# q and k laid out by head channel, and another order of TensorE's work, in a kernel of windowed attention beside a gated MLP

## The chip, the cores and the metric

The kernel runs on one NeuronCore of a Trainium2 chip. The core has five engines, each with its own instruction stream: TensorE (PE; its weight loads are listed apart as PEld), VectorE (DVE), ScalarE (ACT), GpSimd (POOL) and SyncE (SP). Each engine runs its stream in order and waits for others on semaphores. Transfers are issued from the queues of SP, ACT and POOL and run on 16 shared DMA engines. The metric is the time of one execution on the device, in microseconds (us). The runs of the kernel before took 208.5 us in the median (208.3 to 209.07, three runs).

## What is computed

`x` holds 2048 tokens of 512 channels in bf16. Two branches of the normalised tokens are added to it:

```python
xn = _layernorm(x)
# A: 32 heads of 16 channels; a token looks at itself and at 7 tokens before it, two apart
q, k, v = split_heads(xn @ wqkv)
logits = einsum('bhsd,bhswd->bhsw', q, kg) * 16 ** -0.5   # kg: k at s, s-2, ..., s-14
o = einsum('bhsw,bhswd->bhsd', softmax(mask(logits)), vg)
A = o @ wo
# B: a gated MLP that mixes over tokens
z = gelu(xn @ w_in)                                        # 512 -> 1376
z1, z2 = z[..., :688], _layernorm(z[..., 688:])
g = einsum('ts,bsf->btf', w_sp, z2) + b_sp                 # 2048 x 2048
B = (z1 * g) @ w_out                                       # 688 -> 512
out = x + A + B
```

## The kernel before

The tokens are taken in 16 tiles of 128. The program is written with its order by hand: a list of short names for TensorE and ScalarE (`ten`, L418) and one for VectorE (`vec`, L411), which a small loop (`advance`, L604) goes through in order, pulling from the other list what a name needs. Each engine's stream comes out in that order.

*Token tiles.* `s` takes the statistics of a tile (L163), `r` or `R` the inverse root (on POOL, L167, or on ACT for the first two), `n` normalises on VectorE (L175). Tiles 0 to 3 are turned by TensorE (`T`, L180, copied out at L181), tiles 4 to 15 by a DMA transpose from the SP queue (`t`, L184). The result is `xnT`, channels on partitions.

*z2 and z1.* `z` projects a token tile to the second half of z (L190: eight matmuls of 128x344 into a buffer `mm`, of which there are three, two PSUM banks each), `h` is its gelu on ScalarE with a running sum (L196), `q` its square on ScalarE (L201). `zs` makes mean and inverse root for four tiles (L207 to L211), `zn` normalises a z2 tile on VectorE (L217). `y` is a z1 tile: the same L190 and a gelu at L222.

*q and k.* `k` projects chunks (L230): eight matmuls of 128x128 weights on 512 tokens for two of the four groups of channels of q or of k. A partition then holds one of four channels of a head, so a head's 16 channels lie on four partitions and in four groups of the free dimension. ACT copies them out (L232).

*Logits.* For each half `th` of the tokens and each pair of window offsets `w2`: `m` multiplies q by k shifted by the offset (L262, two operations of 4096 elements per partition), `f` and `p` add the four groups (L263, L264; for some pairs the first add is a DMA with accumulation from POOL, `d`, L270), and `S` sums over the four partitions of a head on TensorE with a selector matrix (L276), copied by ACT into `a_sb` with the scale (L278). Now a partition is (quarter of the tokens, head), 32 heads times 4 quarters.

*Softmax and attention.* `x` maximum and subtraction (L286 to L290), `e` exponential on ACT (L294), `u` sum (L299 to L301), `i` inverse by logarithm and exponential on ACT (L305, L306), `c` scaling (L310). `v` projects v in the layout (quarter, head) at once: 32 columns of weights for one channel of all heads, four such matmuls side by side in the array (L245). `H` copies the last 16 tokens of a quarter to the next one, as halo, by DMA (L250, L251). `a0.0` to `a0.11` and `a1.0` to `a1.11` are attention's products and sums for the two halves on VectorE (L318, L322, L331); `.11` writes the output.

*Mixing, gate, output.* `W` loads and transposes 256 rows of w_sp (L338, SP queue) into one of three buffers. `M` mixes one tile (L345: 32 matmuls), ACT adds the bias (L348) into one of three buffers, `g` multiplies by z1 on VectorE (L353) and issues the transpose of the result from SP (L357, or L359 and L360). `Q0` to `Q3` are the four groups of four output tiles (L385 and L390 for the gated part, L396 for attention); `F` adds x and stores (L401, L402). The first half's output groups come before the second's.

In `ten` four z2 tiles are followed by the projections of q and k of the first half, and then z2 tiles, projections, v, z1 and mixing tiles alternate.

## Time and profile before

| | |
|---|---|
| median of three runs | 208.5 us (208.3 to 209.07) |
| span of the profiled execution | 207.7 us, from the first to the last instruction |
| granted TensorE clock | 1.000 |
| DMA | 29.79 MB, 143 GB/s in the mean |

The profiled execution is one run; its span leaves out what lies before the first and after the last instruction, and the page gives no other time for it. The span stands 0.8 us below the median. In groups of instructions a row reads: line, engine, operation, out<-in, shapes, count, then busy us, mean ns of one, and the idle time of the engine before them with what ended it. Durations of neighbours overlap a little, so the pitch of back-to-back work is read from starts.

### The profile page before, as it was taken

The numbers are of one execution on the slowest core, as the hardware profiler recorded it, in microseconds if no ns is written. First come the engines' busy times: TensorE is split into PE (matmuls) and PEld (weight loads), VectorE is DVE, ScalarE is ACT, GpSimd is POOL, SyncE is SP. The second block draws the span as 40 slices with busy tenths as digits, with TensorE's granted clock in tenths as the row PEclk, the third lists the DMA queues.
The fourth block names the chain that finished last, engine by engine and source line by source line (L and its number), as shares of the span: only waits on it lengthen the run. The fifth ranks groups of instructions, "written<-read, shape, count | busy, mean of one in ns | idle before, by whom it ended". The sixth has DMA issues, their size and how long they took to land.

```text
span 207.7 us, 3772 instructions
## 1 busy us (share of the span) xinstructions
PE 197.3 (95%) x1563; PEld 115.3 (56%) x1563; DVE 177.9 (86%) x188; ACT 95.7 (46%) x147; POOL 26.9 (13%) x58
## 2 busy tenths in 40 slices
PE   7689999999997999969999999999999999999993
PEld 2355555555554666636666666666666664443441
DVE  4589849995969799999999999989979999996243
ACT  3567979999887437658463257211111220000000
POOL 2257660043320211000000000000000000000000
PEclk9999999999999999999999999999999999999999
DMA  5975959999660949159082066095999999212022
GB/s 131 375 230 132 80 110 325 203 246 214 129 131 0 110 95 213 30 68 198 0 189 51 3 137 141 13 192 128 229 202 225 203 297 280 73 50 101 3 101 101
DMA packets 66849, 29.79 MB, mean 143 GB/s; under 512 B 56960, under 2 KB 65376, under 8 KB 66704
## 3 DMA queue, kind: packets, MB, share of 16 engines
q1 hardware_dynamic: 60720, 21.16, 48.2%
q0 software_dynamic: 1520, 5.43, 12.3%
q10 hardware_dynamic: 4592, 2.97, 6.3%
q8 instruction: 12, 0.20, 0.4%
q14 instruction: 5, 0.04, 0.1%
HBM read 10.03 MB, written 2.10 MB: 58 GB/s over the span
## 4 chain that ended last, share of the span: by engine, by line
PE 71%; DVE 17%; DMA 3%; POOL 2%; issue 2%; ACT 1%; ACTq 1%; SPq 1%; DVEq 0%
PE mm L345 36%; DVE prod L262 8%; PE mm L190 8%; PE mm L396 7%; PE mm L230 7%; PE mm L385 6%; PE mm L245 3%; DMA z<-in_A_x_dram 3%; DVE z L262 2%; PE aux L385 2%; DVE z L217 2%; DVE prod L264 2%; DVE prod L263 1%; PE mm L390 1%; POOL zrstd L211 1%
## 5 line engine op out<-in xcount | busy, mean ns | idle before, releaser
L345 PE MATMUL mm<-z,wsp 128*128 128x344 bf16 x512 | 75.8, 309 | 1.0 <-ACT z L222 1.0
L345 PEld LDWEIGHTS <-wsp 128*128 128x128 bf16 x512 | 50.1, 98 | 25.7 <-issue 1.3
L190 PE MATMUL mm<-wts,xnT 128*128 128x344 bf16 x256 | 41.0, 309 | 1.1 <-DMA wts<-in_B_w_in_dram 1.1
L348 ACT ACTIVATE qk<-mm,b_col 128x688 bf16<-128x688 f32 x16 | 13.3, 833 | 49.7 <-PE mm L345 40.4
L318 DVE TENSOR_TENSOR prod<-vp,a_sb 128x4096 bf16<-128x4096 bf16 x16 | 36.0, 2282 | 0.0
L262 DVE TENSOR_TENSOR prod<-qk 128x4096 bf16<-128x4096 bf16 x14 | 31.4, 2284 | 2.5 <-ACT qk L232 2.5
L190 PEld LDWEIGHTS <-xnT 128*128 128x128 bf16 x256 | 24.3, 98 | 16.4 <-issue 3.4
L230 PE MATMUL mm<-xnT,wts 128*128 128x512 bf16 x128 | 29.0, 379 | 0.0
L322 DVE TENSOR_TENSOR prod<-prod,prod 128x8192 bf16<-128x8192 bf16 x6 | 26.5, 4419 | 0.1
L230 PEld LDWEIGHTS <-wts 128*128 128x128 bf16 x128 | 14.4, 113 | 12.3 <-issue 0.2
L232 ACT CAST qk<-mm 128x1024 bf16<-128x1024 f32 x16 | 16.0, 1012 | 3.6 <-PE mm L230 3.6
L401 DVE TENSOR_TENSOR z<-mm,wsp 128x512 bf16<-128x512 f32 x12 | 7.7, 684 | 8.8 <-PE mm L396 5.7
L245 PE MATMUL mm<-xnT,wts 128*32 128x512 bf16 x256 | 15.3, 382 | 0.0
L396 PE MATMUL mm<-wts,xnT 32*128 32x512 bf16 x192 | 14.3, 375 | 0.0
L163 DVE BATCH_NORM_STATS2 stats<-z 128x6 f32<-128x512 bf16 x16 | 10.9, 682 | 3.7 <-DMA z<-in_A_x_dram 3.7
L385 PE MATMUL mm<-wts,qk 128*128 128x512 bf16 x60 | 14.0, 380 | 0.0
L222 ACT ACTIVATE z<-mm 128x688 bf16<-128x688 f32 x16 | 11.7, 744 | 4.1 <-PE mm L190 4.0
L196 ACT ACTIVATE z<-mm 128x688 bf16<-128x688 f32 x16 | 11.9, 742 | 3.0 <-PE mm L190 3.0
L385 PEld LDWEIGHTS <-qk 128*128 128x128 bf16 x80 | 7.6, 98 | 9.9 <-issue 1.3
L201 ACT ACTIVATE z_junk<-z 128x688 bf16<-128x688 bf16 x16 | 12.5, 778 | 0.4
L245 PEld LDWEIGHTS <-wts 128*32 128x32 bf16 x256 | 9.2, 140 | 4.5 <-issue 0.9
L396 PEld LDWEIGHTS <-xnT 32*128 32x128 bf16 x256 | 6.4, 93 | 7.8 <-issue 1.3
(79 smaller groups left out, 163.5 us busy)
## 6 DMA issues: line engine op xcount, KB each, us to landing
prod<-prod POOLq DMA_DIRECT2D x6, 512.0 KB, 5.6
wts<-in_A_wo_dram ACTq DMA_DIRECT2D x4, 512.0 KB, 5.7
wsp<-in_A_x_dram SPq DMA_DIRECT2D x2, 1024.0 KB, 7.4
out_dram<-z SPq DMA_DIRECT2D x16, 128.0 KB, 1.7
z<-in_A_x_dram SPq DMA_DIRECT2D x3, 512.0 KB, 4.3
wts<-in_A_wqkv_dram SPq DMA_DIRECT2D x2, 512.0 KB, 7.5
z<-z POOLq DMA_DIRECT2D x2, 512.0 KB, 7.2
wts<-in_B_w_in_dram SPq DMA_DIRECT2D x1, 688.0 KB, 5.7
```

The costliest lines, as they stand in the source:

```text
L190: PE.matmul(pz[:, hh, 0:FHALF], xnT[:, kc, i * P:(i + 1) * P], w_z[part][:, kc, hh * FHALF:(hh + 1) * FHALF], start=(kc == 0), stop=(kc == ...
L201: A.activation(z2_junk[:], z2[:, i, :], ACT.Square, accum_out=zsq[:, i:i + 1])
L230: PE.matmul(pq[:, cc, :], w_c[:, kc], xnT[:, kc, t0:t0 + D], start=(kc == 0), stop=(kc == C - 1))
L232: A.copy(qk[b // 2][:, a, 2 * c2:2 * c2 + 2, o:o + D], pq[:])
L245: PE.matmul(pv[32 * g:32 * g + 32, dd, :], w, r, start=(kc == 0), stop=(kc == C - 1), tile_position=(0, 32 * g))
L262: ops.append(lambda ww=ww, k=k: V.tensor_tensor(pr[:, ww], q, k, ALU.mult))
L318: return lambda: V.tensor_tensor(dst, vp[:, :, th, off:off + GS], a_sb[:, th, w].unsqueeze(1).broadcast_to([P, DH, GS]), ALU.mult)
L322: return lambda: V.tensor_tensor(dst, dst, x, ALU.add)
L345: PE.matmul(pg[:, hh, 0:FHALF], w[:, k, (j % 2) * P:(j % 2 + 1) * P], z2[:, k, hh * FHALF:(hh + 1) * FHALF], start=(k == 0), stop=(k == NT ...
L348: A.activation(g.rearrange("p (a b) -> p a b", a=2), pg[:, :, 0:FHALF], ACT.Identity, bias=b_col[:, j:j + 1])
L385: PE.matmul(po, uT[th][:, m, t0:t0 + P], wout[:, m, :], start=(start and m == 0), stop=(stop and m == MF - 1))
L396: PE.matmul(pos[g], op[32 * g:32 * g + 32, th, d, s * P:(s + 1) * P], wo_r[32 * g:32 * g + 32, d, :], start=(start and d == 0), stop=(stop ...
```

## The change

The whole function is rewritten, but most of its parts compute what they computed. What differs:

- q and k are projected like v: 32 columns of weights for one channel of all heads, four matmuls side by side, so that a partition is (quarter, head) from the start. `k`, `q` and `v` are now eight groups each of 32 matmuls (`heads`), two channels in a group, and each needs all token tiles. In the new lists `q` is the projection, `sq` the square, `kc`, `qc`, `vc` the copies by ACT.
- k gets a halo of 16 tokens by DMA from SP (`kh0` to `kh3`, four channels each); v's halo moves from the ACT queue to SP (`vh`).
- The logits are made for four channels `c` at a time and all eight offsets: `m` two products of 4096 elements, `f` one add (on VectorE, or by DMA from POOL for one of the two product buffers), `p` one add of 2048 for the first channels and two for the others. The head sums, their selector matrix and their copies are gone. The scale moves into the exponential.
- TensorE's order is z2, q and k, z1, v, mixing, output. The z2 tiles 8 to 15 are normalised on ACT (`zn8` to `zn15`), with a bias from VectorE (`zb`).
- Five token tiles are normalised on POOL. w_z of z2 is loaded in two halves; the later loads of x are no longer held back; wk and wq are loaded between the transposes; wy and wv come from POOL at other places.
- The first eight output tiles are copied out of PSUM by ACT (`E`) and then added to x by VectorE (`F`); the stores come last on SP.
- Each of the five engines has a list of its own.

The diff, cut to its core:

```diff
-    def qk_chunks(b, a, c2):
...
-                PE.matmul(pq[:, cc, :], w_c[:, kc], xnT[:, kc, t0:t0 + D], start=(kc == 0), stop=(kc == C - 1))
...
+    def heads(t, w_t, p):
+        for dd in range(2):
+            d = 2 * p + dd
             for kc in range(C):
+                w = w_t[:, kc, :].rearrange("p (h d) -> p h d", d=DH)[:, :, d]
                 for g in range(4):
                     r = xnT[:, kc, :].rearrange("p (t g s) -> p t g s", t=2, g=4)[:, :, g, :]
+                    PE.matmul(t[32 * g:32 * g + 32, dd, :], w, r,
                               start=(kc == 0), stop=(kc == C - 1), tile_position=(0, 32 * g))
...
+    def halo(q, x, d0, d1):
+        for t in range(2):
+            q.dma_start(x[H:P, d0:d1, t, 0:HALO], x[0:P - H, d0:d1, t, GS:GS + HALO])
+        q.dma_start(x[0:H, d0:d1, 1, 0:HALO], x[P - H:P, d0:d1, 0, GS:GS + HALO])
+
+    for c in range(NC):
+        op_(f"kh{c}", [f"kc{2 * c}", f"kc{2 * c + 1}"], lambda c=c: halo(SP, k_v, DC * c, DC * (c + 1)))
...
+    POOLN = (5, 7, 9, 11, 13)
...
+    ZACT = range(8, NT)
+    for i in range(0, NT, 4):
+        op_(f"zs{i}", [f"sq{i + x}" for x in range(4)], lambda i=i: z2_stats(i, 4))
+        op_(f"zr{i}", [f"zs{i}"], lambda i=i: z2_root(i, 4))
+        if i in ZACT:
+            op_(f"zb{i}", [f"zr{i}"], lambda i=i: z2_bias(i, 4))
+    for i in range(NT):
+        g = i // 4 * 4
+        if i in ZACT:
+            op_(f"zn{i}", [f"zb{g}"], lambda i=i: A.activation(
+                z2[:, i, :], z2[:, i, :], ACT.Identity, bias=zbias[:, i:i + 1], scale=zrstd[:, i:i + 1]))
...
+    BUF = {(0, 0): 0, (0, 1): 1, (1, 0): 0, (1, 1): 1, (2, 0): 0, (2, 1): 1, (3, 1): 0, (3, 0): 1}
...
+    def products(c, th):
+        pr = prod[BUF[c, th]].rearrange("p (a w x) -> p a w x", a=2, w=W)
+        for a in range(2):
+            d0 = DC * c + 2 * a
+            k = k_v[:, d0:d0 + 2, th, :]
+            k = bass.AP(k.tensor, k.offset + HALO - DIL * (W - 1), [k.ap[0], [DIL, W], k.ap[1], [1, GS]])
+            q = q_v[:, d0:d0 + 2, th, :].unsqueeze(1).broadcast_to([P, W, 2, GS])
+            V.tensor_tensor(pr[:, a].rearrange("p w (b s) -> p w b s", b=2), q, k, ALU.mult)
...
+    def logits(c, th):
+        pr = prod[BUF[c, th]][:, 0:PU // 2].rearrange("p (w b s) -> p w b s", w=W, b=2)
+        if c == 0:
+            V.tensor_tensor(a_sb[:, th], pr[:, :, 0], pr[:, :, 1], ALU.add)
+        else:
+            V.tensor_tensor(pr[:, :, 0], pr[:, :, 0], pr[:, :, 1], ALU.add)
+            V.tensor_tensor(a_sb[:, th], a_sb[:, th], pr[:, :, 0], ALU.add)
...
+    pe = """wu T0 T1 z0A z1A z0B z1B T2 T3 z2 z3 z4 z5 z6 z7 z8 z9 z10 z11 z12 z13 z14 z15
+        k0 k1 q0 q1 k2 k3 q2 q3 k4 k5 q4 q5 k6 k7 q6 q7 B
+        y0 y1 y2 y3 y4 y5 y6 y7 y8 y9 y10 y11 y12 y13 y14 y15 v0 v1 v2 v3 v4 v5 v6 v7
+        M0 M1 M2 M3 M4 M5 M6 M7 M8 M9 M10 M11 M12 M13 M14 M15
+        gf0 gf1 re0 re1 ao0 ao1 gf2 re2 re3 ao2 ao3""".split() + [f"gf3.{i}" for i in groups[3]]
...
+    act = """sr0 sr1 GL Tc0 Tc1 h0 h1 Tc2 Tc3 h2 h3 h4 h5 h6 sq0 h7 h8 h9 sq1 h10 h11 h12 sq2 h13 h14 sq3 h15
+        kc0 sq4 kc1 sq5 qc0 sq6 qc1 sq7 kc2 sq8 kc3 sq9 qc2 sq10 qc3 sq11 kc4 sq12 kc5 sq13 qc4 sq14 qc5 sq15
+        kc6 kc7 qc6 qc7 Bc yg0 yg1 yg2 yg3 yg4 yg5 yg6 yg7 zn8 yg8 yg9 zn9 yg10 yg11 zn10 yg12 yg13 zn11 yg14 yg15 EL
+        vc0 zn12 vc1 zn13 vc2 zn14 vc3 zn15 vc4 vc5 vc6 vc7
+        G0 G1 e0 G2 i0 e1 i1 G3 G4 G5 G6 LO0 G7 LO1 G8 LO2 G9 LO3 G10 LO4 G11 G12 G13 G14 G15""".split()
+    act += [f"E{i}" for n in (0, 1) for i in groups[n]]
+    dve = """b0 ag0 b1 rc0 n0 ag1 rc1 n1 b2 ag2 b3 ag3 b4 ag4 n2 n3 b5 ag5 b6 ag6 n4 b7 ag7 b8 ag8 n6 b9 ag9 b10 ag10 n8
+        b11 ag11 b12 ag12 n10 b13 ag13 b14 ag14 n12 b15 ag15 n14 n15 zs0 zn0 zn1 zn2 zn3
+        m00 m01 f01 p01 zs4 p00 m10 m11 f11 p11 zs8 p10 zn4 zn5 m20 m21 f21 p21 zs12 zb8 p20 zn6 zn7 zb12
+        m31 m30 f30 p30 X0 p31 u0 C0 X1 g0 g1 a0.0 u1 g2 a0.1 C1 g3 a0.2 g4 a0.3 a0.4 g5 a0.5 a0.6 g6 a0.7 g7 a0.8 a0.9 g8
+        a0.10 g9 a0.11 a1.0 g10 a1.1 a1.2 g11 a1.3 g12 a1.4 g13 a1.5 a1.6 g14 a1.7 g15 a1.8 a1.9 a1.10 a1.11""".split()
+    dve += [f"F{i}" for n in range(4) for i in groups[n]]
+    pool = """b16 gr2 gr4 n5 gr6 n7 gr8 n9 gr10 n11 gr12 n13 gr14 wy zr0 f00 wv zr4 f10 zr8 f20 zr12 f31""".split()
+    sp = """x0 x1 wz0 wz1 x2 x4 x8 x12 t4 t5 wk t6 t7 wq t8 t9 t10 t11 t12 t13 t14 t15 kh0 kh1 kh2 kh3 W0 W1 W2 U0 U1 W3""".split()
+    sp = sp[:-3]
+    sp += """W3 U0 U1 W4 U2 U3 U4 W5 U5 U6 W6 U7 U8 W7 U9 U10 R0 U11 U12 U13 R1 U14 U15""".split()
+    sp.insert(sp.index("W3"), "vh")
+    sp += [f"S{i}" for n in range(4) for i in groups[n]]
```

In the new lists `b` and `ag` are a token tile's statistics, `gr` the inverse root of two tiles, `Tc` the copy of a turned tile, `yg` z1's gelu, `X` and `C` the softmax's maximum and scaling, `G` the bias after mixing, `U` the transposes after the gate `g`, `LO` the loads of wo and w_out, `R` those of x for the output, `S` the stores, `gf`, `re` and `ao` the three parts of an output group, `EL` and `GL` loads of activation tables, and `wu` ten matmuls at the start on zeros, as in the kernel before (L367).

More of the change, by code (lines that the diff above doesn't have):

```diff
@@ L199, in z2_square, with turned, make_T, z_half @@
-    def z2_square(i):
-        A.activation(z2_junk[:], z2[:, i, :], ACT.Square, accum_out=zsq[:, i:i + 1])
-    z2_junk = sb.tile([P, FH], BF16, name="z2_junk")
+    def turned(i, t):
+        A.copy(xnT[:, :, i * P:(i + 1) * P], t[:].bitcast(BF16)[:, 0:D].rearrange("p (c t) -> p c t", c=C))
+    def make_T(i):
+        t = psum("aux", f"T{i}", f"Tc{i}", [f"n{i}"], lambda t: turn(i, t))
+        op_(f"Tc{i}", [f"T{i}"], lambda: turned(i, t))
+    def z_half(t, i, part, hh):
+        for kc in range(C):
+            PE.matmul(t[:, hh, 0:FHALF], xnT[:, kc, i * P:(i + 1) * P], w_z[part][:, kc, hh * FHALF:(hh + 1) * FHALF],
+                      start=(kc == 0), stop=(kc == C - 1))
@@ L293, in softmax_exp @@
[L293 to L304 removed]
+            V.tensor_tensor(lg[0:H, :, 0:HALO], lg[0:H, :, 0:HALO], mask[:], ALU.add)
@@ L615 @@
     with tc.manual_schedule():
-        V.memset(warm, 0.0)
-        idle(10)
-        for n in ten + vec:
+        for n in pe + sum(lists[1:], []):
             advance(n)
```

596 lines of the change are left out of this document (240 added, 356 removed).

## The prediction

> **What bounds the kernel now.** I read the page's busy shares first, then its chain of the work that ended last.
>
> ```profile
> span 207.7 us, 3772 instructions
> ...
> PE 197.3 (95%) x1563; PEld 115.3 (56%) x1563; DVE 177.9 (86%) x188; ACT 95.7 (46%) x147; POOL 26.9 (13%) x58
> ```
>
> TensorE is busy 95% of the span, and VectorE 86%. So there are two full engines, and what matters is how their orders interlock. Next comes the same chain in order of time (start, length, what); its starts give the true pitch of back-to-back work, which a mean duration does not.
>
> ```profile
> 11.77 2.33 PE mm L190 x16
> 14.11 13.83 PE mm L230 x64
> ...
> 29.00 4.49 DVE prod L262 x2
> 33.49 1.48 DVE z L217 x4
> 34.97 2.21 DVE prod L263
> ...
> 38.53 4.40 DVE prod L262 x2
> ...
> 66.08 1.14 DVE prod L264
> ...
> 75.34 0.33 PE aux L276 x4
> 75.67 1.73 PE mm L245 x32
> ...
> 97.69 1.17 PE mm L190 x8
> ...
> 123.79 46.67 PE mm L345 x320
> ...
> 192.37 3.77 PE mm L396 x65
> ...
> 204.38 0.69 DVE z L401
> ```
>
> TensorE's pitches: one z tile 1.17 us; one 32-matmul group of v 1.73; one mixing tile 46.67/10 = 4.67; one head sum 0.33. TensorE is full from 11.77 to 204.38, apart from a few short waits, and 3.3 us follow its last matmul (207.7 - 204.4). VectorE's pitches: one 128x4096 product 2.20, one 128x2048 add 1.14 (1.2 where it waits for the one before), one fold 2.2 to 2.3. The products begin at 29.00, because q and k of the first half are projected right after four z2 tiles (14.11 to 27.94). VectorE's timeline shows how much room this early start leaves:
>
> ```profile
> 91.29 1.22 DVE L299 TENSOR_TENSOR stmp<-a_sb 128x1024 f32<-128x1024 bf16 x1
> ...
> 93.61 4.49 DVE L262 TENSOR_TENSOR prod<-qk 128x4096 bf16<-128x4096 bf16 x2
> ...
> 185.76 2.29 DVE L331 TENSOR_TENSOR xnT<-prod 128x4096 bf16<-128x4096 bf16 x1
> ```
>
> The last attention output is ready at 188.05. TensorE uses it first at 192.37, in the L396 matmuls of the chain above. So VectorE is a mere 4 us ahead of being the bound itself.
>
> **The change part by part.**
>
> *TensorE's work.* The eight head sums go: 8 x 0.33 = 2.6 us less. q and k take the shape of v, 32 matmuls of 128x32 for what were 8 of 128x128. By the rows, 1.73 us against 13.83/8 = 1.73: no change. [...] The weight loads' rows:
>
> ```profile
> L230 PEld LDWEIGHTS <-wts 128*128 128x128 bf16 x128 | 14.4, 113 | 12.3 <-issue 0.2
> ...
> L245 PEld LDWEIGHTS <-wts 128*32 128x32 bf16 x256 | 9.2, 140 | 4.5 <-issue 0.9
> ```
>
> A narrow load takes 140 ns against 113, but 32 of them pass in 1.73 us; if the 27 ns showed on all 512, 13.8 us would come on top and the sum below would be 239. I take the row: nothing.
>
> *The front.* All sixteen z2 tiles now come first, at 1.17 us each, and each needs its token tile. Tiles 4 to 15 come by transposes that SyncE issues:
>
> ```profile
> L184 SPq DMA_TRANSPOSE xnT<-z x12: 1216/1218/1856, 13.5 to 28.9; - x12
> ...
> DMA to landing us min/median/max: 2.3/2.9/6.9
> ```
>
> Their pace, (28.9 - 13.5)/11 = 1.4 us at most and 1.22 at least, now sets TensorE's: z2 and z3 are done near 14.4, t4 starts near 13.9 and lands at 16.8. The loads wk and wq are pushed in between (each an issue of up to 0.7 us, by L250 further down). I put t15's issue at 29.7 (28.7 to 30.7). It lands 2.3 to 6.9 us later; the slowest ones of before ran beside two POOL weight loads, here beside one, so I take 3.9. z15 then ends at 29.7 + 3.9 + 1.2 = 34.8 (32.2 to 38.8). The five normalisations moved to POOL have no row (VectorE's take 0.40 us; up to 1.5 they hide under SyncE's pace), and cost nothing.
>
> *VectorE starts later.* m00 needs k0, k1, q0, q1 (k0 starts at 34.8) and the halo of k, which now goes by DMA. The nearest rows are those of v's halo:
>
> ```profile
> L247 ACT CAST vp<-mm x8: 1012/1012/1014, 54.6 to 87.0; 128x1024 bf16<-128x1024 f32 x8
> ...
> L250 ACTq DMA_DIRECT2D vp<-vp x1: 697/697/697, 88.0 to 88.0; - x1
> L251 ACTq DMA_DIRECT2D vp<-vp x1: 1962/1962/1962, 88.8 to 88.8; - x1
> ...
> DMA to landing us min/median/max: 3.4/3.6/3.8
> ```
>
> Two groups 3.46, the copy 1.0 with some queueing 0.3, a landing of 3.8: m00 = 34.8 + 8.6 = 43.4. The copy of q1 is ready just then too (four groups 6.92, copy 1.0, ScalarE's squares in between 0.5). So the products begin 14.4 us later than at 29.0.
>
> *VectorE's work* up to zb8 in its list: six pairs of products 6 x 4.40 = 26.4; three folds 3 x 2.3 = 6.9; logits, two of one add (2.4) and three of two adds (7.05), where before one add and a head sum did; three z2 statistics, nine operations of the size of L209 with handovers 1.9, and two normalisations 0.74. Sum 45.4, so zb8 starts at 88.8. The new products read q broadcast over the offsets and k in overlapping windows. No row has that shape; the nearest ones agree whatever their runs:
>
> ```profile
> L318 DVE TENSOR_TENSOR prod<-vp,a_sb 128x4096 bf16<-128x4096 bf16 x16 | 36.0, 2282 | 0.0
> L262 DVE TENSOR_TENSOR prod<-qk 128x4096 bf16<-128x4096 bf16 x14 | 31.4, 2284 | 2.5 <-ACT qk L232 2.5
> ...
> L209 DVE SCALAR_TENSOR_TENSOR zvar<-zsq,zvar 128x4 f32<-128x4 f32 x4 | 0.7, 163 | 0.4
> ```
>
> So I take 2.28 (a pitch of 2.20), with 0 to 0.1 more for each.
>
> *The new wait.* Half of the z2 normalisations go to ScalarE as zn8 to zn15, and zn8 waits for zb8. ScalarE works in order: zn8 stands behind yg7, and yg8 behind zn8. TensorE has three mm buffers, so y11 waits for yg8. Without that wait y10 would end at 34.8 + 16 x 1.73 + 0.1 + 11 x 1.17 = 75.5. With it:
>
> ```profile
> L201 ACT ACTIVATE z_junk<-z 128x688 bf16<-128x688 bf16 x16 | 12.5, 778 | 0.4
> ...
> L222 ACT ACTIVATE z<-mm 128x688 bf16<-128x688 f32 x16 | 11.7, 744 | 4.1 <-PE mm L190 4.0
> ```
>
> zb8 (0.16), zn8 (the size of L201, 0.78), yg8 (0.74): y11 starts at 90.5. **TensorE stands still for 15 us.** This is the term that decides. It hardly depends on the front, since k0 moves both ends: 8.6 + 45.4 + 1.7 against 40.7 us after k0.
>
> *After the idle time.* The first matmuls of the kernel, the output stage and VectorE's attention stage, by windows (start:end and length, busy time of PE, PEld, DVE, ACT and POOL with their instructions, granted clock, DMA share, GB/s):
>
> ```profile
> 14.11:27.94 13.83, 13.83 (x65) 7.25 (x64) 11.18 (x34) 10.84 (x17) 9.50 (x23) 1.00 0.78 139
> ...
> 103.80:188.05 84.25, 84.25 (x639) 51.82 (x637) 81.80 (x52) 21.70 (x27) 0.00 (x0) 1.00 0.72 149
> 170.46:204.38 33.92, 33.88 (x352) 14.21 (x350) 24.30 (x21) 0.83 (x1) 0.00 (x0) 1.00 0.39 104
> 1.48:5.30 3.82, 3.74 (x10) 1.23 (x10) 1.90 (x6) 1.21 (x3) 0.68 (x4) 1.00 0.77 187
> ```
>
> Ten matmuls of 512 columns took 3.74 us at the start, where ten of L230 take 2.16: 1.6 us lost, although the granted clock reads 1.00 in both. Before has no long idle time of TensorE inside the kernel, so a restart costs between 0 and 1.6; I take 1.6, as idle TensorE is nearest to its state at the start. [...]
>
> *TensorE's sum.* 90.5 + 1.6 + five z1 tiles 5.8 + v 13.8 + mixing 74.7 + output 33.9 + tail 3.3 = 223.6.
>
> *VectorE's sum.* e0 (the exponential) stands on ScalarE behind G1, so behind M1, which ends at 90.5 + 1.6 + 5.8 + 13.8 + 9.3 = 121.0. G1 (the size of L222) and e0 take 2.8 with their handovers:
>
> ```profile
> L294 ACT ACTIVATE a_sb<-a_sb 128x2048 bf16<-128x2048 bf16 x2 | 3.8, 1911 | 1.2 <-DVE a_sb L290 1.2
> L306 ACT ACTIVATE stmp<-stmp 128x256 f32<-128x256 f32 x2 | 0.8, 417 | 0.1
> L310 DVE TENSOR_TENSOR a_sb<-a_sb,stmp 128x2048 bf16<-128x2048 bf16 x2 | 4.6, 2280 | 0.0
> ```
>
> u0 starts at 123.8. Before was busy for 81.8 us from 103.80 (the end of c0) to 188.05, four final adds (2.4) among it, which now come later. After adds u0 (91.29 to 93.61, so 2.3), a wait for i0 (two of the size of L306 with handovers, 1.3), C0 (2.2) and two gates (0.9): 81.8 - 2.4 + 6.7 = 86.1, and 0.3 for handovers, 86.4. a1.11 ends at 210.2; ao2, ao3 and the last full gated matmuls (2 x 3.46 + 4.33 = 11.2) and the tail 3.3 make 224.7. The later of the two sums decides: 224.7 by the profiled execution's span of 207.7, which lies 0.8 below the median of 208.5. **225.5 us.**
>
> *Nothing, with its cover.* Four table loads fewer and the copies of eight output tiles on ScalarE lie in its idle half; eight of the sixteen final adds leave PSUM's path, but run before the last four. The mixing weights W0 to W2 move on SyncE behind the halos (30 to about 63 us), and M0 needs them at 112. W4 to W7 stand behind the gated transposes:
>
> ```profile
> L338 SPq DMA_TRANSPOSE wsp<-in_B_w_sp_dram x8: 4118/4864/6587, 30.2 to 142.8; - x8
> ...
> DMA to landing us min/median/max: 6.1/7.4/9.2
> ```
>
> W6 stands behind U6, which waits for g6. In VectorE's list u0, C0, X1, u1, C1, seven gates and a0.0 to a0.6 come up to there, 33.6 us by the pitches above: g6 ends at 157.4, two transposes of 1.22 follow, and W6 lands 7.4 later, at 167.2. M12 could start at 121.0 + 10 x 4.67 = 167.7. No cover is left, and the slow ends (6.6, 9.2) would cost up to 5 us by the last of them.
>
> **The rivals.**
>
> *The stall does not arise* (the other side): VectorE reaches zb8 before yg7 is done, so ScalarE never blocks. The sum loses 15.0 + 1.6 and VectorE's chain moves as much: 225.5 - 16.6 = 208.9, the same as before, since the late tokens eat what the head sums gave. It decides from 29 us between m00 and zb8, against 45.4; every 128x4096 pass would have to take 1.1 us. For it speaks L217 (688 elements in 1.48/4 = 0.37 us), which gets near that rate with one tensor operand; against it, all passes of before with two, L262 and L318.
>
> *SyncE becomes the bound in the mixing*: W5 to W7 come late, each behind transposes that wait for VectorE's gates. TensorE then waits before M10, M12, M14, 3 to 5 us more: 229 to 231. For it, the tight sum above; against it, that VectorE sets the end and would be a little ahead.
>
> *An early front and no slow restart*: t15 issued at 28.7 and landing in 2.3, the halo in 3.4: 225.5 - 2.6 - 0.4 - 1.6 = 220.9.
>
> **How the numbers follow.** My forecast 0.72 (its own range 222 to 229), SyncE 0.12, early front 0.10, no stall 0.04, something else 0.02. The front's late end (+4), products of +0.1 each (+1.2 to zb8) and SyncE's 5 us, not all at once, widen the range to 221 to 231.5. Under 0.5% (1 us) a measurement here tells nothing from no change. Slower 0.95; same 0.03 and faster 0.02, both out of the case without a stall.
>
> **What would show it.** In the profile after: the products start at 42 to 46; ScalarE's activation of zn8 waits some 15 us for VectorE; TensorE has one gap of that length in the z1 tiles, near 75 to 90; VectorE waits some 10 us for the first exponential near 112 to 122. Right after the gap matmuls are slower. Wrong would be products under 2 us, no gap, or a z2 stage that ends before 32 or after 39.

## The result and the profile after

The changed kernel takes 266.6 us in the median of four runs (264.7 to 268.0), against 208.5 us before: 1.277 times as long, with a 95% interval of 1.271 to 1.283. The forecast was 225.5 us, in a range of 221 to 231.5. "Slower" was right, the size was not: 41 us are missing. A time below is the median of all executions of a kernel with their range; some executions are slower than the others of the same kernel, so ratios, and comparisons that say "kept", leave out those more than 1.5% above the kernel's fastest.

The page of the changed kernel: the span, the busy shares, TensorE's row of 40 slices of 6.7 us, and the granted clock in the same slices.

```profile
span 266.2 us, 4471 instructions
...
PE 203.4 (76%) x1912; PEld 122.6 (46%) x1915; DVE 179.6 (67%) x179; ACT 95.7 (36%) x152; POOL 36.8 (14%) x46
...
PE   7756959999991000009999999999495889999993
...
PEclk9997979999997555556999999999979799999998
```

VectorE's work is nearly what it was, 179.6 us for 177.9. TensorE's is 203.4 for 197.3, although the head sums are gone: the mean granted clock is 0.894 where before had 1.000, and the slices with a low clock lie in and behind its waits. Most of the 58 us is idle time: TensorE stands for 62.8 us of the span, where it stood for 10.4. In TensorE's row it is one hole of six slices, small dents before it and one behind it. Who waited for whom is in the list of waits, here VectorE's and then TensorE's part (what waited, for whom, us in all, times, the longest):

```profile
DVE prod L322 <- ACT qk L299: 25.5, 1, 25.5
DVE stmp L363 <- ACT a_sb L377: 13.8, 1, 13.8
...
DVE z L164 <- POOL rstd L161: 8.2, 7, 2.1
```

```profile
PE mm L209 <- ACT z L280: 38.2, 1, 38.2
PE mm L426 <- DMA wsp<-in_B_w_sp_dram: 8.1, 3, 3.7
PE mm L209 <- DMA xnT<-z: 7.9, 5, 2.7
```

The stall in z1 is there, at the place that the forecast named (a gelu behind a normalisation that waits for VectorE), but 38 us long and not 15. The products' wait of 25.5 us for a copy by ScalarE was not in the forecast at all. The chain of what ended last gives the order (start, us, what):

```profile
30.23 5.99 DMA xnT<-z
36.27 3.92 PE mm L209 x16
40.19 27.82 PE mm L291 x512
68.03 1.02 ACT qk L299
...
71.28 2.30 DVE prod L322
74.49 10.13 DMA prod<-prod
...
119.21 8.58 PE mm L209 x40
127.79 13.97 PE mm L291 x256
141.76 38.61 PE mm L426 x265
180.37 11.71 DMA wsp<-in_B_w_sp_dram
192.75 14.26 DMA wsp<-in_B_w_sp_dram
```

L291 x512 are all 16 groups of q and k. The copy L299 behind them is the last of the sixteen, and the first product starts only after it. By the order of the lists the first product needs four of them. The rows of the copies, of the products and of the bias (L261, `zb8` and `zb12`) give the starts, first and last:

```profile
L299 ACT CAST qk<-mm x16: 1012/1012/1012, 42.1 to 68.0; 128x1024 bf16<-128x1024 f32 x16
...
L322 DVE TENSOR_TENSOR prod<-qk x16: 2281/2284/2293, 69.1 to 127.6; 128x4096 bf16<-128x4096 bf16 x16
...
L261 DVE SCALAR_TENSOR_TENSOR zbias<-zmean,zrstd x2: 155/160/164, 117.4 to 120.8; 128x4 f32<-128x4 f32 x2
```

With these starts the forecast's path can be set beside the trace, step by step (the last column is the last experiment, told below):

| step | forecast | after | last experiment |
|---|---|---|---|
| q and k begin (k0) | 34.8 | 40.2 | 36.7 |
| k0 to the first product (m00) | 8.6 | 28.9 | 6.9 |
| m00 to zb8 | 45.4 | 48.3 | 49.9 |
| zb8 to y11 | 1.7 | 1.8 | 1.8 |
| y11 to the end | 134.2 | 147.0 | 135.4 |
| span | 224.7 | 266.2 | 230.7 |

The misses are +5.4, +20.3, +2.9, +0.1 and +12.8 us, together 41.5. Half of it is the one wait.

### The profile page after: what moved, and what is told of

Same layout as the page of the kernel before. It is cut to its first block, busy times and chain, and to the rows that moved or that the text cites. A ratio compares the mean times of both kernels' runs of the same rounds, so it can differ in the third digit from the quotient of the medians.

```text
span 266.2 us, 4471 instructions
## 1 busy us (share of the span) xinstructions
PE 203.4 (76%) x1912; PEld 122.6 (46%) x1915; DVE 179.6 (67%) x179; ACT 95.7 (36%) x152; POOL 36.8 (14%) x46
## 4 chain that ended last, share of the span: by engine, by line
PE 51%; DMA 21%; DVE 14%; POOL 7%; issue 4%; ACT 1%; SPq 1%; DVEq 0%; POOLq 0%; ACTq 0%
PE mm L426 19%; PE mm L291 16%; DMA wsp<-in_B_w_sp_dram 14%; DVE prod L322 7%; PE mm L482 5%; PE mm L470 5%; PE mm L209 5%; POOL z L164 4%; DMA prod<-prod 4%; DMA xnT<-z 2%; POOL rstd L161 2%; DMA z<-in_A_x_dram 2%; DVE prod L326 2%; DVE prod L338 1%; PE aux L470 1%
## 5 line engine op out<-in xcount | busy, mean ns | idle before, releaser
L426 PE MATMUL mm<-z,wsp 128*128 128x344 bf16 x512 | 78.4, 317 | 8.1 <-DMA wsp<-in_B_w_sp_dram 8.1
L209 PE MATMUL mm<-wts,xnT 128*128 128x344 bf16 x256 | 44.6, 338 | 47.3 <-ACT z L280 38.2
L426 PEld LDWEIGHTS <-wsp 128*128 128x128 bf16 x512 | 50.9, 100 | 35.6 <-DMA wsp<-in_B_w_sp_dram 9.2
L209 PEld LDWEIGHTS <-xnT 128*128 128x128 bf16 x256 | 26.4, 106 | 64.8 <-issue 38.4
L322 DVE TENSOR_TENSOR prod<-qk 128x4096 bf16<-128x4096 bf16 x16 | 35.6, 2286 | 25.5 <-ACT qk L299 25.5
L291 PE MATMUL mm<-xnT,wts 128*32 128x512 bf16 x768 | 41.9, 380 | 0.0
L387 DVE TENSOR_TENSOR prod<-vp,a_sb 128x4096 bf16<-128x4096 bf16 x16 | 36.1, 2284 | 0.0
L440 ACT ACTIVATE qk<-mm,b_col 128x688 bf16<-128x688 f32 x16 | 13.0, 833 | 59.5 <-PE mm L426 55.7
L291 PEld LDWEIGHTS <-wts 128*32 128x32 bf16 x768 | 28.1, 139 | 13.4 <-issue 0.6
L272 ACT ACTIVATE z<-z,zbias,zrstd 128x688 bf16<-128x688 bf16 x8 | 7.7, 962 | 39.2 <-DVE zbias L261 39.2
L299 ACT CAST qk<-mm 128x1024 bf16<-128x1024 f32 x16 | 16.2, 1012 | 3.2 <-PE mm L291 3.2
L331 POOL DMA_DIRECT2D prod<-prod x8 | 7.3, 1066 | 48.7 <-DVE prod L322 48.7
L154 DVE BATCH_NORM_STATS2 stats<-z 128x6 f32<-128x512 bf16 x16 | 10.8, 676 | 2.9 <-DMA z<-in_A_x_dram 2.9
L363 DVE TENSOR_TENSOR stmp<-a_sb 128x1024 f32<-128x1024 bf16 x2 | 2.4, 1221 | 13.8 <-ACT a_sb L377 13.8
L164 POOL TENSOR_SCALAR z<-z,mv,rstd 128x512 bf16<-128x512 bf16 x5 | 11.0, 2208 | 0.5
```

The source lines that it names most:

```text
L164: eng.tensor_scalar(xn[i % 8], xs[:, i, :], mv[:, i, 0:1], rstd[:, i:i + 1], ALU.subtract, ALU.mult)
L209: PE.matmul(t[:, hh, 0:FHALF], xnT[:, kc, i * P:(i + 1) * P], w_z[part][:, kc, hh * FHALF:(hh + 1) * FHALF], start=(kc == 0), stop=(kc == ...
L291: PE.matmul(t[32 * g:32 * g + 32, dd, :], w, r, start=(kc == 0), stop=(kc == C - 1), tile_position=(0, 32 * g))
L299: op_(f"{a}c{p}", [f"{a}{p}"], lambda: A.copy(dst[a][:, 2 * p:2 * p + 2], t[:].rearrange("p d (t s) -> p d t s", t=2)))
L322: V.tensor_tensor(pr[:, a].rearrange("p w (b s) -> p w b s", b=2), q, k, ALU.mult)
L387: return lambda: V.tensor_tensor(dst, vp[:, :, th, off:off + GS], a_sb[:, th, W - 1 - w].unsqueeze(1).broadcast_to([P, DH, GS]), ALU.mult)
```

## The experiments

**Where the first product's wait comes from.** In the program as built, the first product waits until ScalarE has counted up to its copy of q's channels 14 and 15. That copy writes the two halves of the tokens, 8448 elements apart, in one tile that holds q and k of both: its extent from first to last byte runs over k's first half, which the product reads, but no byte is shared. My theory was that the waits are made from such extents. The first run gives each four channels a region of their own; the copies, the halo and the products take their pieces from these regions.

```diff
-    q_v = qk_all[:, :, 0:DH * GS].rearrange("p t (d s) -> p d t s", d=DH)
-    k_v = qk_all[:, :, DH * GS:].rearrange("p t (d s) -> p d t s", d=DH)
+    qk_c = qk_all[:].rearrange("p (c x) -> p c x", c=NC)
+    q_v = [qk_c[:, c, 0:2 * DC * GS].rearrange("p (t d s) -> p d t s", t=2, d=DC) for c in range(NC)]
+    k_v = [qk_c[:, c, 2 * DC * GS:].rearrange("p (t d s) -> p d t s", t=2, d=DC) for c in range(NC)]
...
```

> Changed kernel, with q and k of four channels each in a region of their own (q, then k, both halves of the tokens), so that no copy of a later group covers the bytes of an earlier one from its first to its last. Nothing else is changed. Theory A (the first product waits for the copy of q's last group because the extents of the copies overlap, and for no data it needs): the first product starts near 49 instead of 69.1, when its halo has landed (48.5), 20 us earlier; the stall of TensorE in z1 falls from 38 to about 18 us, and the time to 246 us (243 to 250). Rival B (the copies are where the wait is booked, but the products are held by halos, by VectorE or by TensorE's rate, and the stretch behind them has waits of its own): the time stays above 261.

248.0 us (246.4 to 249.9), 18.5 less than the changed kernel. The products' row and the bias's row of this run (lines are shifted by six or two):

```profile
L328 DVE TENSOR_TENSOR prod<-qk x16: 2282/2285/2294, 45.9 to 111.1; 128x4096 bf16<-128x4096 bf16 x16
...
L263 DVE SCALAR_TENSOR_TENSOR zbias<-zmean,zrstd x2: 157/160/164, 100.9 to 104.4; 128x4 f32<-128x4 f32 x2
```

The first product starts at 45.9 in place of 69.1, zb8 at 100.9 in place of 117.4, and TensorE's stall falls from 38.2 to 22.8 us. In the program as built the product's wait is now for the copy of q's channels 0 and 1. Theory A holds in the wait and in the time; the product came 3 us earlier than the 49 expected, and the stall was 22.8 us and not about 18. Only the place of the bytes was changed (and one small memset became four), so the wait was for no data. Of the 23.2 us that the first product gained, 16.5 reached zb8: the stretch between them grew from 48.3 to 55.0 us, because VectorE now waits 8.9 us in it for adds that DMAs make (2.7 in the changed kernel), 8.1 of them at once:

```profile
DVE prod L344 <- DMA prod<-prod: 8.1, 1, 8.1
```

**How much the order of ScalarE costs.** The second run leaves that wait, and puts all gelus of z1 and the copies of v ahead of `zn8` to `zn15`.

```diff
-        ... yg6 yg7 zn8 yg8 yg9 zn9 yg10 yg11 zn10 yg12 yg13 zn11 yg14 yg15 EL
-        vc0 zn12 vc1 zn13 vc2 zn14 vc3 zn15 vc4 vc5 vc6 vc7
+        ... yg6 yg7 yg8 yg9 yg10 yg11 yg12 yg13 yg14 yg15 EL
+        vc0 vc1 vc2 vc3 vc4 vc5 vc6 vc7 zn8 zn9 zn10 zn11 zn12 zn13 zn14 zn15
```

> Changed kernel, with ScalarE's order alone changed: all 16 gelus of z1 and the copies of v stand ahead of the eight normalisations of z2. Theory A: the products still wait until 69, but TensorE no longer stalls in z1; it does z1 and v until about 105 and then waits for the last normalisation, zb8 at 117.4 plus 4 for the second bias plus 5 to 8 for the normalisations: mixing starts near 127 instead of 141.8, the time is about 252 us (249 to 257), and the 13.8 us that VectorE waited for the first exponential go with it. Rival: the stall hides under VectorE's own chain and the time falls by less than 4 us.

248.3 us (248.0 to 248.6): 18.3 less, and 0.7 us below the theory's range. The waits of VectorE and TensorE show the mechanism: the products are as late as they were, but TensorE no longer stands in z1 (L209). It stands in the mixing (L426), for VectorE's normalisations of z2 (L275) and for ScalarE's bias copies (L440).

```profile
DVE prod L322 <- ACT qk L299: 25.2, 1, 25.2
```

```profile
PE mm L426 <- DVE z L275: 16.9, 2, 16.5
PE mm L426 <- ACT qk L440: 9.5, 2, 6.8
```

**GpSimd's normalisations.** The third run takes tiles 5, 7, 9, 11 and 13 back to VectorE, with their names in its list.

```diff
-    POOLN = (5, 7, 9, 11, 13)
+    POOLN = ()
...
```

> Changed kernel, with the five token tiles that GpSimd normalised back on VectorE. Theory A (GpSimd, 2208 ns for each and its inverse roots behind them, paces the token tiles): the projections of q and k start 4 to 6 us earlier than 40.2, the first product follows, and the time is 260 to 263 us. Rival (the tiles are paced by the transposes' issue or landing, or by z2's matmuls): the start moves by under 1.5 us and the time by under 2.

262.3 us (260.7 to 264.5), 4.3 less; q and k begin at 36.9 instead of 40.2. The theory's time holds, its start of 4 to 6 us is missed by 0.7. The reason stands in the changed kernel's groups, the same operation and shape on two engines:

```profile
L164 POOL TENSOR_SCALAR z<-z,mv,rstd 128x512 bf16<-128x512 bf16 x5 | 11.0, 2208 | 0.5
```

```profile
L164 DVE TENSOR_SCALAR z<-z,mv,rstd 128x512 bf16<-128x512 bf16 x11 | 4.5, 425 | 8.3 <-POOL rstd L161 8.2
```

2208 ns against 425, and the next inverse root waits behind each in GpSimd's queue: VectorE's 8.2 us of waits.

**The parts together.** First the edits of the first two runs, then those of all three.

> The regions of the first run and the order of ScalarE of the second together. If both waits are separate parts of one chain (products late, so normalisations late, so mixing late), the first product is near 49, zb8 near 97, mixing starts near 107 and the time is about 232 us (228 to 237), VectorE then being the bound. If the two are the same loss, the time is near the better of the two alone, 246 or above.

228.2 us (224.3 to 233.5): the first two add, 266.6 - 18.5 - 18.3 being 229.8. The executions lie on both sides of that sum.

> The regions, the order of ScalarE and the normalisations on VectorE together (what the first three runs did apart). If the three parts stand one behind the other, the 4 us of the third come off the 228.2 us of the first two: 224 us (222 to 226). Rival: with VectorE now the bound, the five normalisations that come back to it (5 x 0.4 us) and its work in front cost what the earlier start gives, and the time stays within 1.5 us of 228.

230.8 us (227.0 to 233.1), above the theory's 226 and about 1 us beyond what the rival allows. The ranges of the two overlap by most of their length; the third part's 4 us are not to be seen here, and why they are not stays open. Executions of one kernel now lay up to 9 us apart, where the changed kernel's lay 3.3.

**The loads of w_sp in SyncE's list.** This goes back to the changed kernel with one list altered.

```diff
-    sp += """W3 U0 U1 W4 U2 U3 U4 W5 U5 U6 W6 U7 U8 W7 U9 U10 R0 ...
+    sp += """W3 W4 U0 U1 W5 U2 U3 U4 W6 U5 U6 W7 U7 U8 U9 U10 R0 ...
```

> Changed kernel, with SyncE's list alone changed: each load of w_sp from the fifth on stands two or three transposes of the gate earlier. Theory (the three waits of the mixing for w_sp, 8.1 us, come from loads that stand behind transposes that wait for VectorE): most of them go and the time is 258 to 262 us. Rival (the loads are slow because of what runs beside them, or VectorE holds the end): the waits stay or another takes their place, and the time moves by less than 2 us.

258.8 us (256.2 to 261.4), 7.8 less, about as much as the waits for w_sp had been (8.1). None of them is left; 3.0 us of waits for ScalarE's bias copies came in their place. In size that is the rival of the prediction which was given 3 to 5 us and 12%.

**Three parts, and four.** The same order, with the regions and the normalisations on VectorE, and then with ScalarE's order too.

> Changed kernel with three of the parts together: the regions, the normalisations on VectorE and the order of the loads of w_sp, but ScalarE's order as in the changed kernel, so with the stall in z1 that the prediction counted. Theory (these are the steps in which the forecast of 225.5 us failed, worth 18.5, 4.3 and 7.8 us alone, and they add): 266.6 - 30.6 = 236 us, or less by what they share, and the stall of TensorE in z1 is 15 to 20 us. Rival (the sum was wrong elsewhere by as much): above 241.

239.2 us (232.0 to 242.8). One execution lies 4 us under the sum, the other three 3 to 7 us above it, so neither theory nor rival is out.

> Regions, ScalarE's order, normalisations on VectorE, and the order of the loads of w_sp together. In the run without the last part TensorE's waits in the mixing were 4.3 us for ScalarE and 3.8 for w_sp, with VectorE busy to the end; theory (VectorE is the bound there, and its products start at 43 and not at 29 as before): 222 to 231 us, no more than 4 us below that run. Rival (the loads are still on the chain): 8 us less, as in the run with the order of the loads alone, near 220.

221.3 us (220.4 to 223.9), 1.053 times before (1.043 to 1.062). Against the three parts without the order (230.8) that is 9.5 us less, and 7.6 by the executions kept (228.2 and 220.6): the rival's size and not the theory's, though that run's profile showed only 3.8 us of waits for w_sp; its profiled execution was the fastest of its four.

**The adds left to DMAs.** Each `fold_dma` of the last kernel becomes the add on VectorE, and its name moves to VectorE's list.

```diff
-        op_(f"f{n}", [f"m{n}"], lambda c=c, th=th: (fold_dma if BUF[c, th] == 0 else fold)(c, th))
+        op_(f"f{n}", [f"m{n}"], lambda c=c, th=th: fold(c, th))
...
```

> The kernel of the run before with all eight first adds on VectorE: no add is left to a DMA with accumulation. VectorE gets four adds of 2.29 us more, 9.2 us, and loses its waits for these DMAs (5.0 us in the run with three parts, 8.0 in the one with two). Theory (VectorE is the bound): 1 to 5 us slower than the run before. Rival (the transfers, 4 MB that run beside the loads of wv and w_sp, hold other loads up): faster by 2 us or more.

224.4 us (223.8 to 225.2), 3.1 slower than the run before (3.8 by the executions kept): as the theory has it. VectorE's busy time grows from 180.8 to 189.8 us, and its waits for these DMAs go, 7.7 us in the profile of the run before, which was that kernel's slowest execution. The DMAs are worth it, if not by much.

**Products before all tokens are there.** In the kernel with three parts VectorE's products begin at 43 us, where before has 29. In the next runs q and k are projected for each half of the tokens apart, so that the first half needs eight token tiles. The kernel that this starts from is the one with regions, ScalarE's order and VectorE's normalisations (230.8 us), without the order of the loads of w_sp; "the run before" in the next text is that one. All five lists are rewritten for it, with ScalarE's normalisations of z2 from `zn8` on among the last gelus of z1, so what it gains is not the halves' alone.

```diff
+    def heads_half(t, w_t, c, th):
+        tv = t[:].rearrange("p a (b s) -> p (a b) s", b=2)
...
+                    r = xnT[:, kc, :].rearrange("p (t g s) -> p t g s", t=2, g=4)[:, th, g, :]
...
-    pe = """... z7 z8 z9 z10 z11 z12 z13 z14 z15 k0 k1 q0 q1 k2 k3 ...
+    pe = """... z7 k00 q00 z8 k10 q10 z9 z10 k20 q20 z11 z12 k30 q30 z13 z14 z15 k01 q01 k11 ...
```

> The kernel of the run before, with q and k projected for each half of the tokens apart (16 groups of 64 matmuls with 256 tokens instead of 16 groups of 32 with 512), the groups of the first half among z2's tiles 8 to 15, and the products of the first half first; the lists of the engines follow that. Theory (what is left over before is that no product can start until all 16 token tiles are there: by 47 us VectorE had done 37.3 us of work in the kernel before and 19.7 in the run with regions and order): the first product starts near 31 and the time is 207 to 215 us, as before within 3 per cent. Rival (matmuls of 256 columns cost as much as of 512, or the narrow weights' loads bind them, so that 27.8 us of projections become up to 55): TensorE is the bound and the time stays above 220.

218.6 us (214.4 to 227.0): two executions at the theory's upper end, 214.4 and 215.6, and two at 221.5 and 227.0. The first product starts at 33.5 and not near 31. The rival's reason is out: the 1024 matmuls with 256 columns cost 29.8 us, little more than 512 with 512 (the group of this run; in the changed kernel the 16 groups took 27.82 us):

```profile
L311 PE MATMUL mm<-xnT,wts 128*32 128x256 bf16 x1024 | 29.8, 275 | 1.1 <-issue 1.1
```

**What scatters.** Three more runs of this kind, first with the halo of k issued two transposes earlier (and the statistics of z2 one product earlier in VectorE's list):

```diff
-    sp = """... t10 t11 t12 t13 kh00 t14 t15 kh10 ...
+    sp = """... t10 t11 kh00 t12 t13 t14 t15 kh10 ...
```

> The kernel with the halves of the tokens apart, with the first halo issued two transposes earlier and VectorE's statistics of z2 one product earlier. Its first product waited 7.1 us for the halo and its last normalisations of z2 stood 2.5 us in front of the mixing. Theory (TensorE is the bound there, 199 us busy and some 10 us of waits): 211 to 219 us, 0 to 3 us less than the 214.4 to 227 of that run. Rival (VectorE's chain decides): 5 us or more less, level with before.

230.4 us (225.5 to 235.9), slower by 12 (11.5 by the executions kept), where 0 to 3 faster was expected. Its profiled execution was the longest of the four; there TensorE waited once in the mixing:

```profile
PE mm L455 <- DMA wsp<-in_B_w_sp_dram: 16.1, 1, 16.1
```

SyncE's timeline of it shows where the load was late: one transpose of the gate (L461) was 10.69 us in issue, where the line's median is 1.2, and the load of w_sp (L439) stood behind it. Whether the shorter executions of this kernel had the same wait is not shown.

```profile
160.90 10.69 SPq L461 DMA_TRANSPOSE qk<-z  x1
171.68 9.10 SPq L439 DMA_TRANSPOSE wsp<-in_B_w_sp_dram  x1
```

So the loads were put ahead, as in the run with that order alone, first in the kernel with halves, then in the one with the earlier halo:

> The kernel with the halves of the tokens apart, with the order of the loads of w_sp of the run with that part alone. Theory (the runs of 214 to 227 us of the kernel without it scatter because a load of w_sp lands late behind slow transposes in SyncE's queue): the median is 211 to 215 us and the runs lie within 4 us; TensorE, with 199 us of work, stays the bound, so it does not get below 208. Rival (the scatter is of the chip or of the clock): the runs lie as far apart as before, with a median near 218.

> The kernel of the run that was slower (earlier halo, statistics earlier, 230 us) with the order of the loads of w_sp alone changed. Theory (its 16.1 us wait in the mixing for w_sp was the whole loss): 210 to 215 us, no more than 2 us from the run beside it. Rival (the earlier halo itself holds up the transposes of the token tiles, and the late mixing comes from there): 220 us or more.

223.2 us (220.8 to 225.6) and 221.1 us (219.2 to 221.7). The executions now lie 4.8 and 2.5 us apart instead of 12.5 and 10.4, near what the theory said. It is not the whole cause of scatter: the run with three parts and this order had 10.8, and the kernel before, measured beside that run, had 6.5 (208.2 to 214.7). The medians did not come to 211 to 215, and the first is 4.6 above the kernel without the order, 7.2 by the executions kept (222.2 and 215.0): here the order of the loads did not help, and it seems to cost. The rival's figure for the second, 220 or more, came out, but not its reason: with the loads in this order the earlier halo costs nothing against the first. The wait had moved to ScalarE, whose timeline (of the first of the two) has it:

```profile
161.60 0.40 ACTq L479 DMA_DIRECT2D wts<-in_B_w_out_dram  x1
170.41 0.81 ACTq L481 DMA_DIRECT2D wts<-in_B_w_out_dram  x2
171.32 2.28 ACT L469 ACTIVATE qk<-mm,b_col 128x688 bf16<-128x688 f32 x3 [13.65 <-DMA qk<-z]
```

The load of the last rows of w_out (L481, two transfers) is issued from ScalarE's queue at 170.41, 8.4 us after the issue before it had ended, and the trace names a transpose that SyncE issued (`qk<-z`) as what ended ScalarE's wait of 13.65 us. In the program as built each of the two transfers waits for one of those transposes, with which it shares no data. Three bias copies (L469) stand behind the load, and TensorE's buffers behind them (5.8 us of TensorE's waiting).

**The loads of the output weights early.** All five are moved to the front of the mixing, when nothing of the gate is under way: in the kernel with halves, earlier halo and w_sp ahead, in the one with four parts, and in the changed kernel alone. The diff is that of the last two; in the first `e0` and `i0` stand earlier in the list.

```diff
-        G0 G1 e0 G2 i0 e1 i1 G3 G4 G5 G6 LO0 G7 LO1 G8 LO2 G9 LO3 G10 LO4 G11 G12 ...
+        LO4 G0 LO0 G1 LO1 e0 G2 LO2 i0 e1 i1 G3 LO3 G4 G5 G6 G7 G8 G9 G10 G11 G12 ...
```

> The kernel with halves, earlier halo and earlier loads of w_sp (221.1 us), with ScalarE's loads of the output weights moved from among the 7th to 12th bias copies to the first four, right behind v. Theory (these loads wait in ScalarE's queue for transposes that SyncE issued, and the bias copies and TensorE behind them): ScalarE's wait of some 13 us goes, TensorE's work (199.6 us) plus some 11 us of waits and start sets the time, 209 to 214 us. Rival (VectorE's gate is late in any case and the transposes with it): no more than 3 us less, 218 or above.

> The same move in the kernel with four parts (221.3 us), where ScalarE stood 10.2 us behind a transpose and TensorE 6.8 us behind ScalarE. Theory: 214 to 219 us; it stays above the one with halves by VectorE's late start. Rival: within 2 us of 221.

> The same move in the changed kernel, alone. There TensorE waited 8.1 us for loads of w_sp, which stood behind transposes and beside the loads of the output weights. Theory (the loads of the output weights are part of that loss): 258 to 264 us. Rival (only the order of the loads of w_sp matters): within 2 us of 266.6.

215.6 us (213.8 to 218.5), 220.0 (217.7 to 222.0) and 255.7 (255.0 to 256.9). In the changed kernel alone this takes 10.9 us off, 2.3 beyond the theory's range, and no wait for w_sp is left there either, although SyncE's list is the old one. In the kernel with halves it takes 5.5, which lies between theory and rival; in the one with four parts 1.3, within the rival's 2.

With 215.6 us this kernel with halves has the lowest median: 1.030 times before (1.027 to 1.034). It does not beat before. By the executions kept it is level with the first kernel with halves (215.3 and 215.0); what it has over that one is that its executions lie 4.7 us apart and not 12.5. The early loads in that first kernel, without the two steps between, were not tried. VectorE's work in the first 47 us tells most of the rest; the windows of before, of the kernel with three parts (regions, ScalarE's order, no normalisations on GpSimd), and of this one (start:end, length, busy us of PE, PEld, DVE, ACT, POOL):

```profile
0.00:47.00 47.00, 42.98 (x229) 23.48 (x230) 37.27 (x72) 35.45 (x62) 18.85 (x47) 1.00 0.88 204
```

```profile
0.00:47.00 47.00, 36.74 (x354) 21.97 (x358) 25.28 (x67) 30.01 (x64) 10.02 (x26) 1.00 0.58 133
```

```profile
0.00:47.00 47.00, 39.77 (x662) 27.93 (x663) 34.53 (x69) 29.03 (x55) 12.67 (x28) 1.00 0.73 156
```

VectorE is 12.0 us behind before with z2 ahead of all of q and k, and 2.7 with halves. Over the whole span it has 2.9 us more to do than before (180.8 against 177.9). The two make 5.6 us, and the profiled spans are 213.2 and 207.7, 5.5 apart; that the two explain it is an argument from one profile, not tried by itself.

**Does the sum close?** The last run is the kernel that the forecast had in mind: regions, VectorE's normalisations, loads of w_sp and of the output weights early, but ScalarE's order as in the changed kernel.

> Changed kernel with the regions, the normalisations on VectorE, the order of the loads of w_sp and the early loads of the output weights, and with ScalarE's order of gelus and normalisations as in the changed kernel, so with the stall in z1: the kernel that the forecast had in mind. Theory (the forecast failed in these steps and in no other of size): 225 to 232 us, with a stall of 18 to 21 us where the forecast had 15. Rival (something else of 8 us or more is missing from the sum): 234 or above.

233.2 us (231.3 to 235.7), 1.2 above the theory's range and under the rival's by 0.8; the stall was 17.7 us, just under the 18 to 21 expected. That is 1.115 times before, so "slower" held without the waits that the forecast had not seen; but it is still 7.7 us above the forecast and 1.7 beyond its range. Its rows for q and k, products and bias, and TensorE's timeline at y11:

```profile
L293 PE MATMUL mm<-xnT,wts x768: 379/379/434, 36.7 to 116.3; 128*32 128x512 bf16 x192
...
L328 DVE TENSOR_TENSOR prod<-qk x16: 2282/2285/2293, 43.6 to 103.7; 128x4096 bf16<-128x4096 bf16 x16
...
L263 DVE SCALAR_TENSOR_TENSOR zbias<-zmean,zrstd x2: 157/159/161, 93.5 to 96.9; 128x4 f32<-128x4 f32 x2
```

```profile
95.30 7.40 PE L211 MATMUL mm<-wts,xnT 128*128 128x344 bf16 x40 [17.70 <-ACT z L282]
```

These fill the last column of the table above: +1.9, -1.7, +4.5, +0.1 and +1.2 us against the forecast. They make 6.0 us of span. One step of size is left, m00 to zb8; 3.9 us of it are waits for adds by DMA.

## Why the prediction was wrong in size, point by point

- **"m00 needs k0, k1, q0, q1 (k0 starts at 34.8) and the halo of k".** This is the step that failed. It took what the lists name for what the instruction waits for. The built wait was for the last copy of q, so that m00 came 28.9 us after k0 and not 8.6. It cost 20.3 us on the path, and 18.5 us of the time when removed alone. That the wait went with the layout alone is shown; that the extent of the copy is what makes it is read off the program and fits, but only this one layout was tried. The prediction's own sign of this was "the products start at 42 to 46": they started at 69.1.
- **"Up to 1.5 they hide under SyncE's pace, and cost nothing".** A bound without a row, too low: 2208 ns measured. k0 came 5.4 us late, at 40.2, which the prediction had named as a sign of being wrong ("a z2 stage that ends ... after 39"). The last transposes landed at 36.2 (30.23 + 5.99 in the chain) for 33.6 assumed, and two z2 tiles still stood behind them, 3.92 us at a granted clock of 0.63, where the forecast had one of 1.2. With the normalisations taken back k0 begins 3.3 us earlier, and 4.3 us of the time go. In the last run 1.9 us are left; TensorE waited there 6.3 us for transposes, in three waits, where the changed kernel has 7.9 in five. The slow matmuls that the prediction put behind the stall come in the front of the changed kernel too: behind waits of 2.62 and 2.71 us two z2 tiles took 4.18 and 3.92 us, at granted clocks of 0.59 and 0.63, for 2.33 before. There they were put at nothing.
- **m00 to zb8, 45.4.** The products were priced right: 2286 ns each for 2284 before, so broadcast and overlapping windows cost nothing to be seen here. What was missed is VectorE's wait for adds that a DMA makes: 2.7 us after, 0.8 and 3.1 us in the last run. Three folds were counted for VectorE and three left to DMAs at no price; the first of these landed 10.13 us after its issue, in the chain above.
- **The stall at y11.** The mechanism was right to the buffer: gelu behind normalisation behind zb8, and 1.8 us from zb8 to y11 for 1.7. Its length follows from the term before: 38.2 us for 15, and 17.7 in the last run.
- **"It hardly depends on the front, since k0 moves both ends".** Borne out by the third run, where the stall stays at 37.8 us with an earlier front. It was the middle that moved.
- **After the idle time.** 1.6 us were taken for the restart. With the five z1 tiles behind it that made 7.4 us; the last run took 7.40, the changed kernel 8.58, so 2.7 us there. The granted clock was low while TensorE stood; windows of the changed kernel within the hole and behind it (busy PE, PEld, DVE, ACT, POOL, then the clock):

```profile
100.00:119.00 19.00, 0.00 (x0) 0.00 (x0) 18.73 (x18) 1.43 (x2) 6.31 (x6) 0.50 0.29 55
119.00:142.00 23.00, 22.79 (x299) 14.30 (x299) 20.63 (x18) 19.12 (x24) 3.62 (x3) 0.88 0.25 47
```

- **"W4 to W7 stand behind the gated transposes ... up to 5 us".** The rival's waits came beside the forecast instead of in its place: 8.1 us, 7.8 us of the time when removed by order. Its reason was right only in part. SyncE issues there with hardly a gap from 163 to 222 us, so by the profile it seldom waits for a gate; what was slow are the loads of w_sp themselves, 10.5 us from issue to landing in the median and 14.3 at most, where the prediction took 7.4 and 9.2 from before, and transposes of up to 5.3 us in issue between them. The mixing took 86.7 us (141.8 to 228.5) where the sum has 74.7: beside the waits its matmuls were slower, 317 ns in the mean for 309 before. That is most of the 12.8 us that the table misses behind y11. The rival's chance was put at 12%, beside a sum that left it no cover. That the loads of the output weights are a second way into the same loss (10.9 us when moved alone) the prediction did not see: it named no work that hides them.
- **TensorE's price of the narrow projections.** Nothing, as the row said: 512 matmuls in 27.82 us, 16 groups of 1.74.
- **The chances.** The four cases of the forecast all assumed the dependencies of the lists. The true case, a wait that no list names, had no place but the 0.02 of "something else". L217, named for the case without a stall, does not get near its rate: 688 elements in 0.37 us are 0.54 ns each, as are L262's 4096 in 2.20; 1.1 us would be 0.27.
- **A small term of the sum.** It takes 2 x 1.73 = 3.46 us for an attention group of the output; the chain of before that it shows reads 3.77 (L396 x65), and so does the chain after. That is 0.6 us for two groups.

What the change gave are the head sums, 2.6 us of TensorE. What it took for them, besides the order, are adds on VectorE, in the groups of the changed kernel:

```profile
L339 DVE TENSOR_TENSOR a_sb<-a_sb,prod 128x2048 bf16<-128x2048 bf16 x6 | 7.3, 1225 | 0.2
L338 DVE TENSOR_TENSOR prod<-prod 128x2048 bf16<-128x2048 bf16 x6 | 7.3, 1223 | 0.1
...
L336 DVE TENSOR_TENSOR a_sb<-prod 128x2048 bf16<-128x2048 bf16 x2 | 2.5, 1226 | 2.7 <-DMA prod<-prod 2.7
```

Fourteen adds, 17.1 us, stand where before has eight (L264, 9.7 us). The work has moved from one nearly full engine to the other.

## What to carry to other kernels

The wait of a step counts before its price (here 25.5 us for products of 2.29): take it from the built program and not from the list of what the step needs, above all where one tile holds pieces that several engines write and read. An order in which one engine does all of a kind first makes the later kind wait for the last item (the products began at 43 us with all of z2 first, at 29 before), and the idle time of an engine that is nearly full (here VectorE's first 47 us) was not given back, as far as the windows above show it. The queues coupled what has nothing to do with each other: a load in the queue of an engine that also copies (ScalarE's wait of 13.65 us), or behind transposes (TensorE's 16.1 us for w_sp behind one of 10.69 us in issue), is best placed where nothing it can be queued behind is late.

## What the hardware showed that I had not expected

- GpSimd took 2208 ns for a 128x512 bf16 operation with two operands per partition, 5.2 times VectorE's 425 (L164 of the changed kernel).
- The issue of one transpose of the gate on SyncE took 1.2 us in the median, and up to 10.69 us (L461 in the run with the earlier halo). The load of w_sp behind it was issued that much later.
- The halo of k, 12 KB from SBUF to SBUF, was on the chain for 2.06 us (first run, four channels), less than v's 3.4 to 3.8 before (16 channels).
- Behind a wait of 2.71 us for a transpose two z2 tiles took 3.92 us at a granted clock of 0.63, and behind one of 2.62 us two took 4.18 at 0.59 (the changed kernel), where such a tile takes 1.17 in before.
